# Attention four heads at a time in a fused attention, MoE and soft-MoE kernel

## The chip, the cores and the metric

The kernel runs on one core of one Trainium2 chip. The metric is device microseconds of one execution; three runs of the kernel before gave 681.8, 683.8 and 684.83, median 683.8.

## The reference

Three layers follow one another; the output of each is the input of the next:

```
# attention: batch 4, 12 heads, 448 positions, 64 wide
scores = cap * tanh(scale * q @ k.T / cap);  scores -= max(scores)
attn = exp(scores);  attn /= sum(attn) + 1e-9;  x = attn @ v      # -> 1792 tokens x 768
# MoE: 768 -> 2048 -> 768
h = x @ w_in;  g = s * relu(h)**2 + b;  x = g @ w_out
# soft MoE: 32 slots, 8 experts of 768 -> 1024 -> 768
logits = x @ phi;  d = softmax over tokens;  c = softmax over slots
slot_in = d.T @ x;  slot_out[e] = relu(slot_in[e] @ w1[e]) @ w2[e];  out = c @ slot_out
```

w_in and w_out arrive as 64-bit floats and are converted on the chip.

## The kernel before

The run has four stretches. In the **opening** the core computes attention of batch 0 and begins to convert weights. Then come four **blocks**, one for each batch: `block(bi)` multiplies the attention output x of batch bi by w_in (`hidden`, tile `hp`, 16 column chunks of 18 products each, in three terms of a high and a low part for accuracy), squares it, and folds it into the logits `L`, the transposed `g` and the running softmax (`post`, `chain`). Blocks 0 to 2 also carry the attention of the next batch, a step of it between any two pieces of `hidden`; block 3 has none. The **tail** reads 48 MB of expert weights (`wt`) and computes the soft MoE.

Attention works on a *pair* of heads at a time, 24 pairs, six for a batch. A pair has eight steps. Steps 0, 2, 4, 6 call `scores` for one of four chunks of 112 keys: six products into `sc` (two heads on 64 rows each, three terms), then a tanh on ScalarE (ACT) into `e`, and after each second chunk one exp over both chunks. `add` on VectorE (DVE) sums the four chunks of e into `es`, whose row 112 holds the 1e-9 of the denominator. In step 3 of the next pair `weighted` runs: two products of ones with `es` give the sums `Sm` (64 identical rows for each head), eight products of v with e give `U` (64 rows for each head, so the pair fills one bank of 128 rows). DVE then takes the reciprocal of Sm, multiplies U by it into `u`, and `split` writes u as a high part (a cast; on DVE in batch 0, on ACT later) and a low part (a subtraction on DVE) into x. Each fp32 product is two matmul records in the trace, so the eight U products are 16 records. `prep_pair` splits q and k in the same way.

PSUM has eight banks: L one, a shared bank "T" one (`bank`, used in turn by the transposes `tp` and `tw`, the projections `pp` and `pf` and the small tiles of `chain`; ACT or DVE must have copied one user out before PE writes the next), sc two, U one, Sm one, and two more that hold a second sc in the opening and `hp` in the blocks.

The order on each engine comes from a scheduler that starts from the order in the code. Every engine runs its own list in order, so an instruction that waits holds all behind it on that engine.

Of the kernel before, what the change touches and what calls it, by code (L numbers as in the profile page):

```python
# [17 lines left out]
P = 128  # L18
B, H, S, D = 4, 12, 448, 64
NP = H // 2  # L20
CP = 112
NCH = S // CP
DM = H * D
KC = DM // P
FF = 2048
# [9 lines left out]
EPS = 1e-9  # L35
CAP_FAST = 40.0
STEPS = 8
DIRECT = 0
CASTS = NP
LEAD = 4  # L40
U = 256
CU = 768
# [5 lines left out]
def load_qk(nc, io, p, q2, k2):  # L48

    nc.sync.dma_start(q2, io["qT"][p])  # L50
    nc.sync.dma_start(k2, io["kT"][p])


class Body:
    def __init__(self, nc, tc, io, consts, general, f64, wsc, osc):
        self.nc, self.tc, self.io, self.c, self.general = nc, tc, io, consts, general
        self.f64, self.wsc, self.osc = f64, wsc, osc
        self.ws, self.wr = {}, {}
        self.x = {}
        self.qk = {}  # L60
        self.r2 = {}
        self.e = {}
        self.u = {}
# [17 lines left out]
    def load_pair(self, p):  # L81
        if p >= B * NP or p in self.qk:
            return
        nc, io = self.nc, self.io
        if p < 2:
            q2, k2 = self.c["early"][p]
        else:
            q2 = self.ap.tile([P, S], F32, tag="q2", bufs=1, name="q2")
            k2 = self.ap.tile([P, S], F32, tag="k2", bufs=1, name="k2")
            load_qk(nc, io, p, q2, k2)  # L90
        v = self.ap.tile([CP, 2, NCH * D], F32, tag="v", bufs=3, name="v")
        nc.sync.dma_start(v, io["v"][2 * p:2 * p + 2].rearrange("i p d -> p i d"))
        self.qk[p] = (q2, k2, v)

    def prep_pair(self, p):
        if p >= B * NP:
            return
        q2, k2, v = self.qk[p]
        t = [self.ap.tile([P, S], F32R, tag=n, bufs=2, name=n) for n in ("qh", "ql", "kh", "kl")]
        self.split(t[0], t[1], q2, p)  # L100
        self.split(t[2], t[3], k2, p)
        self.qk[p] = (*t, v)

    def scores(self, p, c):

        nc = self.nc
        qh, ql, kh, kl, _ = self.qk[p]
        sc = (self.ps2 if self.ps2 is not None and c % 2 else self.psa).tile([CP, 2, 512], F32, tag="sc", bufs=1, name="sc")
        for j, (k, q) in enumerate(((kh, qh), (kh, ql), (kl, qh))):
            for i in range(2):  # L110
                r = slice(64 * i, 64 * i + 64)
                nc.tensor.matmul(sc[:, i, :S], k[r, c * CP:(c + 1) * CP], q[r, :], start=(j == 0), stop=(j == 2))  # L112
        if c % 2 == 0:
            self.e.setdefault(p, []).append(self.ap.tile([CP, 2, 2, S], F32, tag="e", bufs=3, name="e"))
        nc.scalar.activation(self.e[p][-1][:, :, c % 2, :], sc[:, :, :S], AF.Tanh, scale=self.c["tsc"][:CP])  # L115

    def chunk(self, g, c):

        return self.e[g // 2][c // 2][:, g % 2, c % 2, :]

    def greatest(self, g):
        nc, c = self.nc, self.c
# [17 lines left out]
    def expo(self, p, c):  # L140

        ready = [] if c % 2 == 0 else self.e[p][c // 2:]
        if self.general:
            ready = self.e[p] if c == NCH - 1 else []
            for i in range(2 if ready else 0):
                self.greatest(2 * p + i)
        for e in ready:
            self.nc.scalar.activation(e, e, AF.Exp, scale=self.c["acap"][:CP])  # L148

    def add(self, p, half):  # L150

        nc, es, e = self.nc, self.es[:CP], self.e[p][half]
        if half == 0:
            nc.vector.tensor_add(es, e[:, :, 0, :], e[:, :, 1, :])
        else:
            for k in range(2):
                nc.vector.tensor_add(es, es, e[:, :, k, :])  # L157

    def weighted(self, p):

        nc, c = self.nc, self.c
        U = self.psa.tile([P, 512], F32, tag="U", bufs=1, name="U")
        Sm = self.psa.tile([P, 512], F32, tag="S", bufs=1, name="Sm")
        v = self.qk[p][-1]
        for k in (3, 2, 1, 0) if p < DIRECT else ():
            for i in range(2):
                nc.tensor.matmul(Sm[64 * i:64 * i + 64, :S], c["ones"][:CP, :64], self.chunk(2 * p + i, k), start=(k == 3), stop=False)
        for i in range(2):
            nc.tensor.matmul(Sm[64 * i:64 * i + 64, :S], c["ones"][:CP + 1, :64], self.es[:CP + 1, i, :], start=(p >= DIRECT), stop=True)  # L169
        for k in range(NCH):  # L170
            for i in range(2):
                nc.tensor.matmul(U[64 * i:64 * i + 64, :S], v[:, i, k * D:(k + 1) * D], self.chunk(2 * p + i, k),  # L172
                                 start=(k == 0), stop=(k == NCH - 1))
        del self.qk[p], self.e[p]
        rec = self.ap.tile([P, S], F32, tag="rec", bufs=1, name="rec")
        nc.vector.reciprocal(rec, Sm[:, :S])  # L176
        u = self.ap.tile([P, S], F32, tag="u", bufs=1, name="u")
        nc.vector.tensor_mul(u, U[:, :S], rec)  # L178
        xt = self.xtile(p // NP)
        self.split(xt[:, 0, p % NP, :], xt[:, 1, p % NP, :], u, p)  # L180

    def xtile(self, bi):
        if bi not in self.x:
# [3 lines left out]

    def attention(self):

        for p in range(2):  # L190
            self.load_pair(p)
        self.prep_pair(0)
        self.es = self.ap.tile([P, 2, S], F32, name="es")
        self.nc.vector.memset(self.es, EPS)
        if not self.general:
            self.nc.vector.tensor_scalar(self.es, self.es, self.c["eps"], None, op0=ALU.mult)
        self.nc.vector.memset(self.es[:CP], 0.0)
        last = B * NP
        for p in range(last + 1):
            for k in range(STEPS):  # L200
                if p < last and k % 2 == 0:
                    if k == 0:
                        self.load_pair(p + 1)
                    self.scores(p, k // 2)
                    self.expo(p, k // 2)
                elif k == 3 and p:
                    self.weighted(p - 1)
                elif k in (5, 7) and p < last:
                    if p >= DIRECT and (k == 7 or not self.general):
                        for h in range(2) if self.general else (k // 7,):  # L210
                            self.add(p, h)
                    if k == 5:
                        self.prep_pair(p + 1)
                yield

    def convert(self, units):

# [65 lines left out]
    def conv_units(self):  # L283
# [510 lines left out]
def layouts(inputs):  # L794
    import numpy as np
    cc = np.ascontiguousarray
    q, k, v = inputs["q"], inputs["k"], inputs["v"]
# [18 lines left out]
    r = np.arange(P)  # L816
# [31 lines left out]
```

## Time and profile before

| | |
|---|---|
| median of three runs | 683.8 us |
| span of the profiled execution | 677.3 us |
| median of the runs over that span | 6.5 us |
| PE busy | 626.0 us (92%) |
| ACT busy | 416.2 us (61%) |
| DVE busy | 386.0 us (57%) |
| DMA reads and writes | 200 GB/s over the span |

The profile gives no time for its own execution beside the span, so the 6.5 us that lie around it are taken from the median. The averages hide that the stretches differ: the rows below give the engines' work by stretch.

### The profile page before, as it was taken

To read this page: it belongs to the slowest core of one execution; us is meant where nothing else is said; L and a number is where in the kernel's file an instruction comes from. 1 tells how busy PE (TensorE), PEld (TensorE's weight loads), DVE (VectorE), ACT (ScalarE), POOL (GpSimd) and SP (SyncE) were. 2 spreads that over 40 slices of the span, in tenths; PEclk is the share of its full clock that TensorE was granted. 3 is DMA by queue.
4 is the path that set the end of the run, shared out by engine and by line. 5 is a ranking of instruction groups with operands and counts; after the bars stand their busy time and mean duration, and the time that the engine had idled before them with its cause. 6 is when DMAs were issued, how large, how long until landed. Compare 5 with 4: busy or idle time off the path is not lost.

```text
span 677.3 us, 10643 instructions
## 1 busy us (share of the span) xinstructions
PE 626.0 (92%) x4234; PEld 403.8 (60%) x4234; DVE 386.0 (57%) x574; ACT 416.2 (61%) x688; POOL 4.0 (1%) x11
## 2 busy tenths in 40 slices
PE   4878999999999999999999999999999988987883
PEld 2323566666566666566566666667868864436773
DVE  6999998998785675745455655654332214101121
ACT  5959788986896877587768677776645550010011
POOL 1000000000000000000000000000000000000000
PEclk9979999999999999999999999999999998998887
DMA  7534468678485633132232232111977728999998
GB/s 230 195 101 144 153 246 289 219 271 280 172 276 198 215 98 107 51 94 80 74 99 74 75 91 72 46 47 47 370 269 282 274 92 337 420 419 417 418 412 309
DMA packets 43720, 136.55 MB, mean 202 GB/s; under 512 B 4352, under 2 KB 21264, under 8 KB 36752
## 3 DMA queue, kind: packets, MB, share of 16 engines
q1 hardware_dynamic: 43376, 135.28, 55.6%
q8 instruction: 35, 0.57, 0.4%
q0 software_dynamic: 288, 0.53, 0.2%
q14 instruction: 21, 0.17, 0.1%
HBM read 117.70 MB, written 18.09 MB: 200 GB/s over the span
## 4 chain that ended last, share of the span: by engine, by line
PE 69%; DMA 14%; DVE 10%; ACT 4%; issue 2%; SPq 0%; DVEq 0%
PE hp L385 32%; DMA wt<-in_w_dram 11%; PE U L172 10%; PE sc L112 8%; PE tp L400 4%; PE Sm L169 3%; DVE rec L176 2%; PE pt L474 2%; PE L L414 2%; PE tw L334 2%; DVE es L157 2%; DVE o L264 1%; ACT e L148 1%; PE si_ps L658 1%; PE idle L502 1%
## 5 line engine op out<-in xcount | busy, mean ns | idle before, releaser
L385 PE MATMUL hp<-x,ws 128*128 128x448 f32 x1152 | 278.1, 380 | 0.0
L385 PEld LDWEIGHTS hp<-x,ws 128*128 128x128 f32 x1152 | 204.3, 188 | 54.3 <-issue 40.5
L370 DVE TENSOR_TENSOR ws<-wr,ws 128x384 fp32r<-128x384 f32 x128 | 70.3, 554 | 99.7 <-ACT ws L369 96.7
L115 ACT ACTIVATE e<-sc,c_tsc 112x896 f32<-112x896 f32 x96 | 96.2, 1010 | 22.5 <-PE sc L112 22.1
L172 PE MATMUL U<-e,v 112*64 112x448 f32 x384 | 88.1, 552 | 9.9 <-DVE u L178 6.8
L369 ACT CAST ws<-wr 128x384 fp32r<-128x384 f32 x128 | 65.1, 514 | 37.8 <-PE hp L385 37.6
L148 ACT ACTIVATE e<-e,c_acap 112x1792 f32<-112x1792 f32 x48 | 86.2, 1797 | 0.4
L176 DVE RECIPROCAL rec<-Sm 128x448 f32<-128x448 f32 x24 | 70.9, 2954 | 16.3 <-PE Sm L169 15.3
L172 PEld LDWEIGHTS U<-e,v 112*64 112x64 f32 x384 | 29.5, 138 | 56.2 <-issue 48.3
L157 DVE TENSOR_TENSOR es<-es,e 112x896 f32<-112x896 f32 x48 | 52.2, 1087 | 18.3 <-ACT e L148 18.1
L402 ACT COPY g<-tp 112x256 f32<-112x256 f32 x128 | 42.0, 376 | 20.4 <-PE tp L400 19.7
L112 PE MATMUL sc<-qh,kh 64*112 64x448 f32 x192 | 46.0, 461 | 8.7 <-DVE kh L73 6.5
L390 ACT ACTIVATE r<-hp 128x448 f32<-128x448 f32 x64 | 34.6, 541 | 25.6 <-PE hp L385 25.4
L112 PEld LDWEIGHTS sc<-qh,kh 64*112 64x112 f32 x192 | 17.8, 176 | 44.2 <-issue 21.0
L400 PE MATMUL tp<-c_cst,r 128*112 128x128 f32 x256 | 38.9, 275 | 1.4 <-ACT r L391 1.2
L112 PE MATMUL sc<-ql,kh 64*112 64x448 f32 x192 | 39.5, 382 | 0.0
L722 ACT COPY wt<-op 128x512 f32<-128x512 f32 x12 | 7.0, 586 | 52.7 <-PE op L717 52.7
L112 PE MATMUL sc<-qh,kl 64*112 64x448 f32 x192 | 39.1, 381 | 0.4 <-DVE kl L74 0.4
L701 PE MATMUL so_ps<-wt,free 128*32 128x128 f32 x768 | 29.8, 303 | 10.0 <-DMA wt<-in_w_dram 10.0
L391 ACT ACTIVATE r<-r 128x448 f32<-128x448 f32 x64 | 37.3, 584 | 0.4
L400 PEld LDWEIGHTS tp<-c_cst,r 128*112 128x112 f32 x256 | 29.5, 133 | 10.5 <-ACT g L402 2.2
L701 PEld LDWEIGHTS so_ps<-wt,free 128*32 128x32 f32 x768 | 24.7, 122 | 14.1 <-DMA wt<-in_w_dram 12.7
(138 smaller groups left out, 581.8 us busy)
## 6 DMA issues: line engine op xcount, KB each, us to landing
wt<-in_w_dram SPq DMA_DIRECT2D x48, 1024.0 KB, 14.2
wr<-wsc SPq DMA_DIRECT2D x48, 384.0 KB, 3.1
raw<-in_w_in_dram SPq DMA_DIRECT2D x16, 768.0 KB, 4.4
raw<-in_w_outT_dram SPq DMA_DIRECT2D x16, 768.0 KB, 5.3
wsc<-wr SPq DMA_DIRECT2D x16, 384.0 KB, 3.2
osc<-o SPq DMA_DIRECT2D x24, 256.0 KB, 3.1
wt<-osc SPq DMA_DIRECT2D x6, 1024.0 KB, 7.3
v<-in_v_dram SPq DMA_DIRECT2D x24, 224.0 KB, 2.7
```

The source lines that it names most:

```text
L112: nc.tensor.matmul(sc[:, i, :S], k[r, c * CP:(c + 1) * CP], q[r, :], start=(j == 0), stop=(j == 2))
L115: nc.scalar.activation(self.e[p][-1][:, :, c % 2, :], sc[:, :, :S], AF.Tanh, scale=self.c["tsc"][:CP])
L148: self.nc.scalar.activation(e, e, AF.Exp, scale=self.c["acap"][:CP])
L157: nc.vector.tensor_add(es, es, e[:, :, k, :])
L172: nc.tensor.matmul(U[64 * i:64 * i + 64, :S], v[:, i, k * D:(k + 1) * D], self.chunk(2 * p + i, k), start=(k == 0), stop=(k == NCH - 1))
L176: nc.vector.reciprocal(rec, Sm[:, :S])
L369: self.nc.scalar.copy(hi, u)
L370: self.nc.vector.tensor_sub(lo, u, hi.bitcast(F32))
L385: nc.tensor.matmul(hp[:, :S], ws[kc // 3][:, w, kc % 3, :], x[:, s, kc, :], start=(k == 0), stop=(k == 3 * KC - 1))
L400: self.nc.tensor.transpose(tp[:CP, q * P:(q + 1) * P], r2[:, q * CP:(q + 1) * CP], self.c["idn"])
L402: self.nc.scalar.copy(self.g[q][:CP, :, fc * P:(fc + 1) * P], tp[:CP, 2 * q * P:2 * (q + 1) * P].rearrange("p (a b) -> p a b", b=P))
L701: nc.tensor.matmul(so_ps[32 * e:32 * e + 32, G, :], ht[G][:, f, 32 * e:32 * e + 32], w2[e // 2][:, e % 2, f, :], start=(f == 0), stop=(f = ...
```

## The change

Attention works on a *quad* of four heads, 12 quads, three for a batch, with 16 steps each.

- U is [128, 2, 512], two banks. Each head has 32 rows in each bank: its 64 columns of v are cut in two halves of 32. A quad has 32 U products of 32 columns in place of 2 x 8 of 64; the first two key chunks run at step 9, the last two in step 3 of the next quad. The rows of x are thereby in another order, and w_in's rows are laid out to match on the host.
- Sm is one tile for four heads, 32 rows each: four products of 32 columns in place of 2 x 2 of 64, and one reciprocal [128, 448] in place of two. Its own bank is gone; it uses the shared bank T. From quad 3 on ACT copies Sm out of T and the reciprocal works in place in SBUF.
- `finish`: U is multiplied by the reciprocal in place in PSUM, [128, 2 x 448] in one instruction; the high part is always cast by ACT from PSUM, [128, 896]; the low part is one subtraction of that size.
- e is one tile per key chunk, [112, 4 heads, 448], with three buffers as before; exp has the same size as before, and `add` is three instructions of 1792 in place of six of 896.
- es is set by GpSimd (POOL) instead of DVE. Pair 1's casts go to ACT. The split q and k have three buffers instead of two.

On DVE, in the opening, from a reciprocal on. Before (names: es sums of exp, x the output of attention, o and wr converted weights, ws split weights):

```order
L176 RECIPROCAL rec<-Sm 128x448
L154 TENSOR_TENSOR es<-e 112x896
L178 TENSOR_TENSOR u<-U,rec 128x448
L73 CAST qh<-q_313 128x448
L73 CAST x_273<-u 128x448
L74 TENSOR_TENSOR ql<-q_313,qh 128x448
L74 TENSOR_TENSOR x_273<-u,x_273 128x448
L73 CAST kh<-k_314 128x448
L157 TENSOR_TENSOR es<-es,e 112x896
L74 TENSOR_TENSOR kl<-k_314,kh 128x448
L157 TENSOR_TENSOR es<-es,e 112x896
```

Now, for four heads:

```order
L175 RECIPROCAL rec<-Sm 128x448
L75 TENSOR_TENSOR kl<-k_328,kh 128x448
L199 TENSOR_TENSOR U<-U,rec 128x2x448
L423 TENSOR_TENSOR ws<-wr,ws 128x384
L158 TENSOR_TENSOR es<-e 112x1792
L75 TENSOR_TENSOR x_371<-U,x_371 128x896
L74 CAST qh<-q_405 128x448
L74 CAST kh<-k_406 128x448
L75 TENSOR_TENSOR ql<-q_405,qh 128x448
L158 TENSOR_TENSOR es<-es,e 112x1792
```

One such row of rec, U and x now stands for two before, and the cast of x has left the engine.

On PE, in a block. Before, a pair's sums and products stand together (hp is the MoE product, tp a transpose into bank T):

```order
L400 MATMUL tp<-c_cst,r_1519 112x128 x4
L385 MATMUL hp<-x_894,ws 128x448 x2
L169 MATMUL Sm<-es,c_ones 64x448 x2
L172 MATMUL U<-e,v 64x448 x8
L385 MATMUL hp<-x_894,ws 128x448 x6
```

Now a quad's Sm stands in the row of users of bank T:

```order
L453 MATMUL tp<-c_cst,r_880 112x128 x4
L115 MATMUL sc<-qh,kh 112x448
L115 MATMUL sc<-ql,kh 112x448 x2
L115 MATMUL sc<-qh,kl 112x448
L172 MATMUL Sm<-es,c_ones 32x448 x4
L115 MATMUL sc<-qh,kl 112x448
L438 MATMUL hp<-x_371,ws 128x448 x3
L453 MATMUL tp<-c_cst,r_944 112x128 x4
```

and some runs of U are broken by other products:

```order
L189 MATMUL U<-e,v 32x448 x9
L369 MATMUL pp<-o,c_misc 32x256 x6
L189 MATMUL U<-e,v 32x448 x4
L387 MATMUL tw<-c_cst,o 128x128 x4
L189 MATMUL U<-e,v 32x448 x3
```

The Sm of a quad waits for tp before it to be copied out, and the tp behind it waits for the copy of Sm; and 9, 4 and 3 aren't multiples of four. In blocks 0 to 2 five runs of U are broken so by products that aren't Sm; before, three runs were.

The diff, cut to its core:

```
-    def split(self, hi, lo, src, p):
-        (self.nc.vector.tensor_copy if p < CASTS else self.nc.scalar.copy)(hi, src)
+    def split(self, hi, lo, src, vector):
+        (self.nc.vector.tensor_copy if vector else self.nc.scalar.copy)(hi, src)
...
+        t = [self.ap.tile([P, S], F32R, tag=n, bufs=2 if self.general else 3, name=n) for n in ("qh", "ql", "kh", "kl")]
+        self.split(t[0], t[1], q2, p < CASTS and p != 1)
...
+        if j == 0:
+            self.e.setdefault(Q, []).append(self.ap.tile([CP, 4, S], F32, tag="e", bufs=4 if self.general else 3, name="e"))
+        nc.scalar.activation(self.e[Q][c][:, 2 * j:2 * j + 2, :], sc[:, :, :S], AF.Tanh, scale=self.c["tsc"][:CP])
...
+    def add(self, Q, c):
+        es, e = self.es[:CP], self.e[Q]
+        self.nc.vector.tensor_add(es, e[0] if c == 1 else es, e[c])
...
+            self.Sm = self.psl.tile([P, 512], F32, tag="L", bufs=1, name="Sm") if direct else self.bank("Sm")
...
+        for i in range(4):
+            nc.tensor.matmul(self.Sm[32 * i:32 * i + 32, :S], c["ones"][:CP + 1, :32], self.es[:CP + 1, i, :], start=not direct, stop=True)
+        rec = self.ap.tile([P, S], F32, tag="rec", bufs=1, name="rec")
+        if Q < NQ:
+            nc.vector.reciprocal(rec, self.Sm[:, :S])
+        else:
+            nc.scalar.copy(rec, self.Sm[:, :S])
+            nc.vector.reciprocal(rec, rec)
...
+            self.U = self.psa.tile([P, 2, 512], F32, tag="U", bufs=1, name="U")
+        for k in chunks:
+            for h in range(2):
+                for i in range(4):
+                    nc.tensor.matmul(self.U[32 * i:32 * i + 32, h, :S], self.v[2 * Q + i // 2][:, i % 2, k * D + 32 * h:k * D + 32 * h + 32],
+                                     self.chunk(4 * Q + i, k), start=(k == 0), stop=(k == NCH - 1))
...
+    def finish(self, Q):
...
+        u = self.U[:, :, :S]
+        nc.vector.tensor_mul(u, u, self.rec[:, None, :].to_broadcast([P, 2, S]))
+        self.split(hi, lo, u, False)
...
+        self.nc.gpsimd.memset(self.es, EPS)
...
+                if not self.general and Q and s in (1, 3) and not (s == 1 and Q - 1 < DIRECT):
+                    if s == 1:
+                        self.add(Q - 1, 3)
+                    else:
+                        self.sums(Q - 1, (2, 3))
+                        self.weighted(Q - 1, (2, 3))
+                        self.finish(Q - 1)
...
+            if s == 9:
+                if Q < DIRECT:
+                    self.sums(Q, (0, 1))
+                self.weighted(Q, (0, 1))
+            if s in (9, 13) and Q >= DIRECT:
+                self.add(Q, 1 if s == 9 else 2)
...
+    wi = wi.reshape(NQ, 4, 2, D // 2, FF).transpose(0, 2, 1, 3, 4)
```

DIRECT is 0, so the branches for it don't run. The code for a large cap (`general`) is not taken in these runs.

## Rows read from the trace of the kernel before

**Rows 1.** Busy time of the engines by stretch: stretch, length, busy (instructions), granted clock.

```profile
6.00:81.00 75.00, 61.25 (x320) 27.89 (x321) 71.86 (x93) 57.19 (x57) 0.00 (x0) 0.93 0.51 165
81.00:410.00 329.00, 325.67 (x1849) 206.96 (x1849) 230.27 (x321) 253.28 (x423) 0.54 (x1) 1.00 0.47 157
410.00:555.00 145.00, 143.71 (x803) 107.32 (x801) 58.04 (x90) 91.06 (x183) 0.00 (x0) 1.00 0.45 164
555.00:677.00 122.00, 95.39 (x1270) 61.61 (x1267) 24.19 (x63) 13.15 (x25) 0.54 (x1) 0.86 0.97 391
```

**Rows 2.** DVE in order of time, at the opening's start and end: start, us.

```profile
7.24 0.81 DVE L194 MEMSET es<- 128x896 f32 x1
14.64 1.08 DVE L154 TENSOR_TENSOR es<-e 112x896 f32<-112x896 f32 x1
74.80 2.95 DVE L176 RECIPROCAL rec<-Sm 128x448 f32<-128x448 f32 x1
80.79 0.62 DVE L74 TENSOR_TENSOR x<-u,x 128x448 fp32r<-128x448 f32 x1
```

**Rows 3.** Groups by line and shape: busy us, mean ns, idle before and releaser.

```profile
L176 DVE RECIPROCAL rec<-Sm 128x448 f32<-128x448 f32 x24 | 70.9, 2954 | 16.3 <-PE Sm L169 15.3 <-PE U L172 1.1
L157 DVE TENSOR_TENSOR es<-es,e 112x896 f32<-112x896 f32 x48 | 52.2, 1087 | 18.3 <-ACT e L148 18.1
L178 DVE TENSOR_TENSOR u<-U,rec 128x448 f32<-128x448 f32 x24 | 14.7, 613 | 0.9 <-PE U L172 0.8
L74 DVE TENSOR_TENSOR x<-u,x 128x448 fp32r<-128x448 f32 x24 | 14.9, 621 | 8.0 <-ACT x L73 7.6
L73 DVE CAST x<-u 128x448 fp32r<-128x448 f32 x6 | 2.3, 386 | 0.0
L73 ACT CAST x<-u 128x448 fp32r<-128x448 f32 x18 | 10.1, 564 | 9.2 <-DVE u L178 8.9
L115 ACT ACTIVATE e<-sc,c_tsc 112x896 f32<-112x896 f32 x96 | 96.2, 1010 | 22.5 <-PE sc L112 22.1
L148 ACT ACTIVATE e<-e,c_acap 112x1792 f32<-112x1792 f32 x48 | 86.2, 1797 | 0.4
```

**Rows 4.** POOL in order of time: its last instruction in the opening.

```profile
3.48 0.54 POOL L776 DMA_DIRECT2D c_misc<-in_phi_dram  x1
```

**Rows 5.** The chain that ended last: start, us until the next piece, records.

```profile
302.98 0.90 PE Sm L169 x4
303.89 3.01 PE U L172 x16
308.31 0.89 PE L L414 x8
379.41 3.57 PE pt L474 x32
```

**Rows 6.** PE in order of time around a broken run.

```profile
321.47 0.97 PE L169 MATMUL Sm<-es,c_ones 113*64 113x448 f32 x2
322.37 0.46 PE L112 MATMUL sc<-qh,kh 64*112 64x448 f32 x2
...
323.16 0.59 PE L169 MATMUL Sm<-es,c_ones 113*64 113x448 f32 x1
...
327.07 0.67 PE L385 MATMUL hp<-x,ws 128*128 128x448 f32 x2
```

**Rows 7.** Waits: who for whom, us in total, times, longest us.

```profile
PE U L172 <- DVE u L178: 6.8, 3, 4.8
PEld pf L324 <- ACT o L336: 2.6, 5, 1.1
PEld tp L400 <- ACT g L402: 2.2, 6, 0.4
```

More of the change, by code (lines that the diff above doesn't have):

```diff
@@ L20 @@
 NP = H // 2
+NQ = H // 4
 CP = 112
@@ L62, in __init__ @@
         self.e = {}
-        self.u = {}
+        self.v = {}
         self.nslot = 0
@@ L83, in load_pair, with load_v @@
             return
-        nc, io = self.nc, self.io
         if p < 2:
[L86 to L93, printed above, removed]
+            self.qk[p] = self.c["early"][p]
+            return
+        self.qk[p] = [self.ap.tile([P, S], F32, tag=n, bufs=1, name=n) for n in ("q2", "k2")]
+        load_qk(self.nc, self.io, p, *self.qk[p])
+    def load_v(self, p):
+        if p >= B * NP or p in self.v:
+            return
+        self.v[p] = self.ap.tile([CP, 2, NCH * D], F32, tag="v", bufs=3, name="v")
+        self.nc.sync.dma_start(self.v[p], self.io["v"][2 * p:2 * p + 2].rearrange("i p d -> p i d"))
     def prep_pair(self, p):
@@ L147, in expo @@
         for e in ready:
             self.nc.scalar.activation(e, e, AF.Exp, scale=self.c["acap"][:CP])
[L150 to L154, printed above, removed]
-        else:
[L156 to L180, printed above, removed]
@@ new lines, in add, with sums @@
+    def add(self, Q, c):
+        es, e = self.es[:CP], self.e[Q]
+        self.nc.vector.tensor_add(es, e[0] if c == 1 else es, e[c])
+    def sums(self, Q, chunks):
+        nc, c = self.nc, self.c
+        direct = Q < DIRECT
+        if chunks[0] == 0 or not direct:
+            self.Sm = self.psl.tile([P, 512], F32, tag="L", bufs=1, name="Sm") if direct else self.bank("Sm")
+        for k in chunks if direct else ():
+            for i in range(4):
+                nc.tensor.matmul(self.Sm[32 * i:32 * i + 32, :S], c["ones"][:CP, :32], self.chunk(4 * Q + i, k), start=(k == 0), stop=False)
+        if chunks[-1] != NCH - 1:
+            return
+        for i in range(4):
[3 more added lines that the diff above has]
+            nc.vector.reciprocal(rec, self.Sm[:, :S])
+        else:
+            nc.scalar.copy(rec, self.Sm[:, :S])
+            nc.vector.reciprocal(rec, rec)
+        self.rec = rec
@@ new lines, in weighted @@
+    def weighted(self, Q, chunks):
+        nc = self.nc
+        if chunks[0] == 0:
+            self.U = self.psa.tile([P, 2, 512], F32, tag="U", bufs=1, name="U")
+        for k in chunks:
+            for h in range(2):
+                for i in range(4):
+                    nc.tensor.matmul(self.U[32 * i:32 * i + 32, h, :S], self.v[2 * Q + i // 2][:, i % 2, k * D + 32 * h:k * D + 32 * h + 32],
+                                     self.chunk(4 * Q + i, k), start=(k == 0), stop=(k == NCH - 1))
@@ L182, in xtile @@
+    def finish(self, Q):
+        nc = self.nc
+        xt = self.xtile(Q // NQ)
+        k = 2 * (Q % NQ)
+        hi, lo = (xt[:, s, k:k + 2, :] for s in range(2))
+        u = self.U[:, :, :S]
+        nc.vector.tensor_mul(u, u, self.rec[:, None, :].to_broadcast([P, 2, S]))
+        self.split(hi, lo, u, False)
+        del self.e[Q], self.v[2 * Q], self.v[2 * Q + 1]
     def xtile(self, bi):
@@ L188, in attention @@
     def attention(self):
-        for p in range(2):
-            self.load_pair(p)
+        self.load_pair(0)
+        self.load_pair(1)
+        self.load_v(0)
         self.prep_pair(0)
-        self.es = self.ap.tile([P, 2, S], F32, name="es")
-        self.nc.vector.memset(self.es, EPS)
+        self.prep_pair(1)
+        self.load_v(1)
+        self.es = self.ap.tile([P, 4, S], F32, name="es")
+        self.nc.gpsimd.memset(self.es, EPS)
         if not self.general:
-            self.nc.vector.tensor_scalar(self.es, self.es, self.c["eps"], None, op0=ALU.mult)
@@ L197, in attention @@
[L197 to L213, printed above, removed]
-                yield
+            self.nc.gpsimd.tensor_scalar(self.es, self.es, self.c["eps"], None, op0=ALU.mult)
@@ new lines, in attention @@
+        if DIRECT:
+            self.nc.gpsimd.memset(self.es[:CP], 0.0)
+        last = B * NQ
+        for Q in range(last + 1):
+            for s in range(2 * STEPS):
+                if Q < last:
+                    if s % 2 == 0:
+                        c, j = divmod(s // 2, 2)
+                        self.scores(2 * Q + j, c)
+                        if j:
+                            self.expo(Q, c)
+                    self.between(Q, s)
+                if not self.general and Q and s in (1, 3) and not (s == 1 and Q - 1 < DIRECT):
[5 more added lines that the diff above has]
+                        self.finish(Q - 1)
+                yield
@@ new lines, in between @@
+    def between(self, Q, s):
+        if s == 0:
+            self.load_pair(2 * Q + 2)
+        if s == 4:
+            self.load_v(2 * Q + 1)
+            self.load_v(2 * Q + 2)
+        if s == (13 if self.general else 7):
+            self.prep_pair(2 * Q + 2)
+            self.load_pair(2 * Q + 3)
+        if s == 15:
+            self.prep_pair(2 * Q + 3)
+        if self.general:
+            if s == 14:
+                for k in range(1, NCH) if Q >= DIRECT else ():
+                    self.add(Q, k)
+                self.sums(Q, range(NCH))
+                self.weighted(Q, range(NCH))
+                self.finish(Q)
+        else:
[5 more added lines that the diff above has]
+                self.add(Q, 1 if s == 9 else 2)
```

34 lines of the change are left out of this document (16 added, 18 removed).

## The prediction

> **What bounds the kernel now.** I read the busy time by stretch first, since the change touches only attention and the averages of the whole run hide where that stands. The reader is to see three limits in it [rows 1]. In the opening (6 to 81 us) DVE is busy 71.86 of 75 us (96%), PE 61.25, ACT 57.19: DVE is the limit. From 81 to 555 PE is busy 325.67 + 143.71 = 469.4 of 474 us, with DVE at 70% and then 40%: PE is the limit. From 555 on DMA is (0.97 busy). So DVE work counts in the opening, PE work in the blocks; what ends the blocks earlier moves the tail, which starts when they free its buffers, earlier by as much. Second, the timeline of DVE [rows 2]: the last reciprocal of batch 0 starts at 74.80, and the last subtraction into x ends at 80.79 + 0.62 = 81.4; block 0 can't finish its first column chunk without it. Third, the groups by shape for the durations [rows 3], the chain for the pitch of matmul runs [rows 5], and the waits on the PSUM banks [rows 7].
>
> **The opening.** Three quads take the place of six pairs. DVE, from [rows 3], the memset of es from [rows 2]:
> - reciprocals: 3 fewer x 2.954 = -8.9 us;
> - casts of x: 6 x 0.386 = -2.3, to ACT;
> - es is set by POOL: at least two memsets of 0.81 = -1.6;
> - an instruction of twice the columns: 448 to 896 takes the subtraction from 0.621 to the 1.087 of the same-shaped add, so 0.47 for each 448 more. Adds: 18 x 1.087 = 19.6 become 9 x (1.087 + 0.94) = 18.2, -1.3. Multiplications 6 x 0.613 = 3.7 become 3 x 1.08 = 3.2, subtractions 6 x 0.621 = 3.7 become 3 x 1.09 = 3.3: -0.9 together. That a PSUM operand and a PSUM result at 896 cost no more than this no row shows; even 0.5 us on each of the six would be 3 us.
>
> Sum -15. The new order splits one pair more ahead of the boundary, about 1.2 on DVE, so DVE has 71.9 - 14 = 58 us in the opening. ACT gains: three casts [128, 896] from PSUM at about 1.0 (the tanh of that size, 1.01), two casts of pair 1 and two of the extra pair at 0.564 each: 57.2 + 5.3 = 62.5. ACT is then the longest, from 6 us on: no end before 68.5. DVE as the limit lost 4% to waits; two engines near one another lose more, and there is a new hand-over. U is one buffer, and from a quad's last exp it is free only after add 2.0, sums 0.9, reciprocal 2.95, multiplication 1.1, cast 1.0, subtraction 1.1 = 9 us, while ACT has two chunks of the next quad ahead of it, 2 x (2 x 1.0 + 1.8) = 7.6, and a few casts. I count 1 us for each of two hand-overs and 3 us of other waits: the end comes at about 73.5 in place of 81.4. **-8**, bounds: -13 (ACT never waits) and -3 (ACT waits 10 us). Less than the 14 us taken from DVE, because ACT stands right behind it.
>
> POOL's two instructions on es are not in the trace. POOL is free from 4.0 us [rows 4], and the first add into es stood at 14.64 [rows 2] and can't come earlier now, as it needs eight tanhs and two exps where it needed four and one. DVE would need 2 x (0.81 + 0.68) = 3 us; up to 10.6 it costs nothing. I take 0, bounds 0 and +3.
>
> **The blocks.** Quads 3 to 11, nine of them, run where PE is the limit. A pair takes 0.90 + 3.01 = 3.91 us of PE [rows 5], a quad's worth 7.82. The change's shape stands in the trace at two places: L is four products of 32 columns over 448, eight records, in 0.89: so Sm for four heads takes 0.89 where it took 1.80. pt is 16 products of 32 columns, 112 rows and 512 moving columns in 3.57 us; times 448/512 that is 3.12 for 16 products of U, 6.25 for a quad against 6.02. Per quad 7.14 against 7.82: -0.68, times nine **-6.1**.
>
> Whether four column groups keep each other's pace decides this term. In the rows they do [rows 5]: pt's 32 records take 0.112 us each, 0.098 at 448 columns, where a record of the two-group U takes 3.01/16 = 0.188 and one alone would take 0.376. A rule of the Trainium skill speaks against it: "TensorE: Matmul & The Clock Gate", section "Part 3: Packing small matmuls — row/col tiling", says that four packed tiles measured 3.07 times one, and three column tiles 2.38 times. By that page a record would take 0.376/3.07 = 0.122 and the quad more than two pairs, and the estimate for the run would be 686. I take pt's row, whose shape is U's but for the columns; the other case is among the rivals.
>
> Three things are taken off or added.
> - Broken runs. Five of the new U runs are cut at a place that is no multiple of four by other products, against three before. [rows 6] show what a cut costs: Sm and U with scores between them take 327.07 - 321.47 = 5.60, less 0.79 for the scores (322.37 to 323.16) 4.81, against 3.91: 0.90. Two more cuts, less some cuts of Sm that are gone: **+1**, bounds 0 and +5 x 0.9.
> - Bank T. Behind Sm in PE's order stand pf or tp, which wait for ACT's copy of Sm; before it a tp or tw. The nearest rows are PE's waits for copies out of T: 2.6 us in 5 waits for pf, 2.2 in 6 for tp [rows 7], out of some 100 uses. Nine more uses with some 0.1 each: **+1**. From the other side, ACT can be in an exp (1.80) whenever PE gets there; nine times that and the copy (0.55) is 21.
> - PE waited 6.8 us in three waits for u to free U's bank [rows 7], and loses 4.6 in all from 81 to 555 [rows 1]. In the blocks a quad's U begins several hp runs after the former one's subtraction, since six steps of the attention lie between; **-0.5**.
>
> ACT's nine copies of Sm (0.55 each) and its larger casts add 5 us to the 344 of 474 that it is busy, DVE loses some 4 us a quad: neither becomes the limit. The tail has none of it.
>
> **Sum.** -8 - 6.1 + 1 + 1 - 0.5 = -12.6 on the profile's span of 677.3, so 664.7; the three runs lie 6.5 above the span by their median, and I take that as fixed: 671.2, so **671 us**, 1.9% faster.
>
> **Rivals.**
> - *The opening gives back most*: the hand-over of U and ACT's 62 us of work swallow it, and it ends at 78 instead of 73.5. For it speaks that a quad's finishing chain is 9 us against 5 for a pair, and that e has three buffers for four chunks, so a tanh of chunk 3 waits for U; against it the 14 us that DVE, the engine that bound, no longer has to do. -3 - 4.6 = -7.6: 676.
> - *More than that*: ACT hides its waits under the conversion work, -13, and no wait on T, -6: 665.
> - *Four groups don't run abreast in U.* pt uses one weight tile for all four groups; U has four of v and four moving tiles. If only three keep pace, a record takes 0.376/3 = 0.125: U 8.0 and Sm 1.0 are 9.0 a quad, +1.2 instead of -0.68, nine times +10.8. -8 + 10.8 + 1.5 = +4.3: 688, on the edge of what can be told from no change.
> - *The end on the other side: bank T becomes PE's wait.* Sm, tp, tw, pf and pp all go through one bank, and each next user needs ACT, which runs exps of 1.80 in its list. If each of the nine Sm holds PE by 1.8 before and 1.2 behind, that is +27 where I count 1: -12.6 + 26 = +13, 697. It costs the gain from about 1.4 us more for each Sm, and shows as slower from 1.8. Against it: the longest wait of tp for a copy was 0.4 [rows 7], and the new order puts ACT's copy right behind the copies of the tp before it.
>
> **How the numbers follow.** Less than 0.5% (3.4 us) can't be told from no change in runs that spread by 3 us; that is between 680.4 and 687.2. Chances: forecast 0.56, the opening gives back 0.19, more 0.12, four groups not abreast 0.07, bank T 0.06. Of the second some 0.04 lies above 680.4, of the fourth some 0.04 below 687.2. So faster is 0.56 + 0.15 + 0.12 = 0.83, the same 0.08, slower 0.03 + 0.06 = 0.09. The range leaves out the last two cases and the ends of the second and third: 663 to 679. The bounds of the single terms (opening -13 to -3, cuts 0 to +4.5, POOL 0 to +3) lie within it, unless several fall on one side together.
>
> **What would show it.** In the profile after, the opening's end (the last subtraction into x of batch 0) stands near 73.5, with ACT busier than DVE there; twelve reciprocals of 2.95; 32 records of U in 3.1 to 3.2 us of the chain, and 8 of Sm in 0.9; PE still busy over 98% from there to the end of the blocks, and that stretch about 4 to 5 us shorter; the tail as long as now. The prediction is wrong if a run of U takes over 3.5 us, if PE's waits for the copies of Sm or for bank T come to more than 5 us, or if the opening ends after 78.

## The result, and the profile after

The changed kernel takes 690.7 us (median of 4 runs, 688.79 to 692.73) against 682.8 us for the kernel before beside it (4 runs, 679.28 to 684.83): ratio 1.0124, 95% interval 1.0094 to 1.0155. It is 1.2% slower where 1.9% faster was forecast. The profiled execution spans 688.9 us where it spanned 677.3, a difference of 11.6 where the medians give 7.9. In all other runs the time lies 1.7 to 2.0 us above the span, so the trace of the kernel before is of its shortest run (679.28, 3.5 below its median) and that of the changed kernel of one at its median. So the 6.5 us set around the span ahead of the prediction are mostly this difference, and a difference of 2 or 3 us between two single traces may lie between executions and not between kernels.

The busy time by stretch, with stretches moved to where the work now is (columns as in [rows 1]: stretch, length, busy us and instructions of PE, PEld, DVE, ACT, POOL, then granted clock, DMA share and GB/s):

```profile
6.00:83.00 77.00, 60.92 (x415) 25.47 (x415) 64.81 (x68) 61.72 (x64) 5.68 (x2) 0.91 0.58 181
83.00:218.00 135.00, 131.09 (x841) 83.05 (x840) 100.81 (x131) 111.90 (x173) 0.00 (x0) 1.00 0.70 237
218.00:236.00 18.00, 11.87 (x62) 6.86 (x62) 14.17 (x13) 12.26 (x16) 0.00 (x0) 0.76 0.33 102
236.00:422.00 186.00, 184.76 (x1191) 114.55 (x1187) 90.28 (x131) 132.44 (x232) 0.60 (x1) 1.00 0.29 88
422.00:567.00 145.00, 143.36 (x864) 107.38 (x860) 52.70 (x80) 91.62 (x183) 0.00 (x0) 1.00 0.46 165
567.00:689.00 122.00, 91.26 (x1267) 57.44 (x1266) 24.16 (x63) 13.17 (x25) 0.54 (x1) 0.90 0.97 391
```

Two rows stand out. In the opening DVE no longer fills the stretch (64.81 of 77, against 71.86 of 75 in [rows 1]), yet no engine fills it in its place. And there is a stretch of 18 us in which PE is busy for 11.87 and its clock falls to 0.76, inside the blocks, where PE was always full.

To see where time came and went, I take from the timeline the start of the first relu of each block, that is, the moment at which the first `hp` chunk of a batch is done (us):

| kernel | block 0 | block 1 | block 2 | block 3 | span |
|---|---|---|---|---|---|
| before | 85.7 | 222.4 | 361.9 | 481.6 | 677.3 |
| after | 87.1 | 235.6 | 373.3 | 493.2 | 688.9 |
| difference | +1.4 | +13.2 | +11.4 | +11.6 | +11.6 |

At the last chunk of block 0 the difference was still +1.2 (214.6 and 215.8). So, in these two traces, the opening gained nothing, a loss of 12 us stands at the boundary of blocks 0 and 1 (called the stop below), and the rest of the run is as long as it was.

**The opening.** POOL's instructions on es in order of time (start, us; answers [rows 4]):

```profile
5.07 1.59 POOL L218 MEMSET es<- 128x1792 f32 x1 [1.02 <-DVE c_eps L818]
6.76 5.03 POOL L220 TENSOR_SCALAR es<-es,c_eps 128x1792 f32<-128x1792 f32 x1
```

DVE at the start and end of the opening, in order of time (in brackets: idle before, and what ended it; answers [rows 2]):

```profile
5.26 1.65 DVE L74 CAST qh<-c_tmp 128x448 fp32r<-128x448 f32 x1 [0.59 <-DMA c_tmp<-in_qT_dram]
6.83 0.37 DVE L74 CAST kh<-c_tmp 128x448 fp32r<-128x448 f32 x1
7.12 3.85 DVE L75 TENSOR_TENSOR ql<-c_tmp,qh 128x448 fp32r<-128x448 f32 x1
10.89 0.61 DVE L75 TENSOR_TENSOR kl<-c_tmp,kh 128x448 fp32r<-128x448 f32 x1
...
81.68 1.09 DVE L75 TENSOR_TENSOR x<-U,x 128x896 fp32r<-128x896 f32 x1 [1.22 <-ACT x L74]
```

The cast that ran beside POOL's memset took 1.65 us where the same cast otherwise takes 0.37 to 0.39, and the subtraction beside POOL's scaling took 3.85 where it otherwise takes 0.61. Both stand ahead of the first tanh: PE waited 2.96 us for ql within the first scores, and the first tanh started at 12.32 instead of 7.92. x of batch 0 is complete at 81.68 + 1.09 = 82.8, not at 73.5.

**The stop.** The last quad of batch 1, on PE in order of time (the rows of `hp` before 226 and most others are left out):

```profile
192.91 0.62 PE L377 MATMUL pf<-c_cst,c_tmp 128*128 128x32 f32 x4
...
219.01 0.60 PE L453 MATMUL tp<-c_cst,r 128*112 128x128 f32 x4
220.57 0.96 PE L172 MATMUL Sm<-es,c_ones 113*32 113x448 f32 x8
...
226.18 0.46 PE L115 MATMUL sc<-qh,kh 64*112 64x448 f32 x2 [2.41 <-ACT e L118]
...
231.96 1.11 PE L438 MATMUL hp<-x,ws 128*128 128x448 f32 x2 [2.35 <-ACT x L74]
233.34 2.23 PE L438 MATMUL hp<-x,ws 128*128 128x448 f32 x5 [0.27 <-DVE x L75]
```

and what DVE did for that quad:

```profile
189.51 2.01 DVE L158 TENSOR_TENSOR es<-es,e 112x1792 f32<-112x1792 f32 x1
...
226.19 2.95 DVE L178 RECIPROCAL rec<-rec 128x448 f32<-128x448 f32 x1
...
229.87 1.10 DVE L199 TENSOR_TENSOR U<-U,rec 128x896 f32<-128x896 f32 x1
...
232.19 1.09 DVE L75 TENSOR_TENSOR x<-U,x 128x896 fp32r<-128x896 f32 x1
```

es is ready at 191.5, but PE reaches Sm at 220.57: twelve other users of bank T (the first and the last of them are shown; the expectation of the first experiment counts eight) stand ahead of it in PE's list. From Sm on every step is the one that all wait for, and each stands behind other work: ACT copies Sm at 221.92 (behind an exp), DVE starts the reciprocal at 226.19 (behind an add of 2.02 and three conversions) and the multiplication at 229.87 (behind one more), and only then can ACT cast x, at 231.00. x is complete 12.7 us after Sm started, while PE has only scores left, which wait for e, and the first products of block 1, which wait for x. In the kernel before, es of batch 1's last pair was ready at 199.63, Sm stood at 200.35, in a bank of its own, x was complete at 210.6, and block 1 began without a wait (the kernel before, DVE and PE):

```profile
198.55 1.08 DVE L157 TENSOR_TENSOR es<-es,e 112x896 f32<-112x896 f32 x1
200.35 0.97 PE L169 MATMUL Sm<-es,c_ones 113*64 113x448 f32 x4
209.95 0.63 DVE L74 TENSOR_TENSOR x<-u,x 128x448 fp32r<-128x448 f32 x1
```

The clock pays a second time. The stretch in 10 us pieces (columns as above):

```profile
210.00:220.00 10.00, 9.55 (x62) 6.62 (x61) 0.78 (x2) 7.74 (x17) 0.00 (x0) 1.00 0.65 209
220.00:230.00 10.00, 6.10 (x36) 3.09 (x34) 7.70 (x7) 8.35 (x11) 0.00 (x0) 0.87 0.18 58
230.00:240.00 10.00, 7.77 (x36) 3.78 (x36) 7.72 (x9) 4.13 (x8) 0.00 (x0) 0.62 0.60 197
```

After PE's waits the granted clock is 0.87 and then 0.62, and five records of hp take 2.23 us at 233.34 where six take 1.42 at full clock (below). The two pieces hold 3.90 + 2.23 = 6.1 us of idle PE; 6.10 x 0.13 + 7.77 x 0.38 = 3.7 us more, as an estimate, went into a slower clock. That is 9.8 of the 12. The rest is work that stands here in PE's list: from the last relu of block 0 to the first of block 1 PE runs 73 records here, and 45 in the kernel before.

**The durations.** Groups by shape (busy us, mean ns, idle before and releaser; answers [rows 3]):

```profile
L199 DVE TENSOR_TENSOR U<-U,rec 128x896 f32<-128x896 f32 x12 | 13.1, 1092 | 0.2
L74 ACT CAST x<-U 128x896 fp32r<-128x896 f32 x12 | 10.9, 907 | 0.4 <-DVE U L199 0.4
```

The chain that ended last, around an unbroken run of U (start, us until the next piece, records; answers [rows 5]):

```profile
418.48 1.42 PE hp L438 x6
...
420.33 3.14 PE U L189 x32
```

Each single duration came out within 0.1 us of the forecast: 1.09 for the instructions of 896 columns, in PSUM too, 0.91 for ACT's cast (forecast 1.0), 0.53 for the copy, 0.89 from Sm's start to the next product (220.57 to 221.46 above), 3.14 for 32 of U.

### The profile page after: what moved, and what is told of

Its sections match the earlier page's. It is cut to its first block, busy times and chain, and to the rows that moved or that the text cites. A ratio compares the mean times of both kernels' runs of the same rounds, so it can differ in the third digit from the quotient of the medians.

```text
span 688.9 us, 11343 instructions
## 1 busy us (share of the span) xinstructions
PE 623.3 (90%) x4618; PEld 394.7 (57%) x4618; DVE 348.6 (51%) x491; ACT 424.6 (62%) x693; POOL 10.8 (2%) x13
## 4 chain that ended last, share of the span: by engine, by line
PE 63%; DMA 16%; ACT 11%; DVE 5%; issue 3%; SPq 0%; DVEq 0%; ACTq 0%
PE hp L438 30%; DMA wt<-in_w_dram 11%; PE U L189 10%; PE sc L115 7%; PE tp L453 4%; ACT e L118 4%; ACT e L153 3%; PE pt L527 2%; PE L L467 2%; DMA k<-in_kT_dram 1%; DMA raw<-in_w_in_dram 1%; DMA q<-in_qT_dram 1%; PE tw L387 1%; PE si_ps L711 1%; PE Sm L172 1%
## 5 line engine op out<-in xcount | busy, mean ns | idle before, releaser
L189 PE MATMUL U<-e,v 112*32 112x448 f32 x768 | 95.2, 562 | 1.9 <-ACT e L153 1.9
L115 PE MATMUL sc<-qh,kh 64*112 64x448 f32 x192 | 47.6, 470 | 20.2 <-ACT e L118 12.7
L158 DVE TENSOR_TENSOR es<-es,e 112x1792 f32<-112x1792 f32 x24 | 48.5, 2022 | 25.3 <-ACT e L153 25.2
L189 PEld LDWEIGHTS U<-e,v 112*32 112x32 f32 x768 | 25.2, 113 | 48.3 <-issue 42.1
L115 PE MATMUL sc<-ql,kh 64*112 64x448 f32 x192 | 41.0, 389 | 3.0 <-DVE ql L75 3.0
L115 PE MATMUL sc<-qh,kl 64*112 64x448 f32 x192 | 41.3, 386 | 0.7 <-DVE kl L75 0.7
L754 PE MATMUL so_ps<-wt,free 128*32 128x128 f32 x768 | 27.9, 283 | 13.6 <-DMA wt<-in_w_dram 13.6
L178 DVE RECIPROCAL rec<-rec 128x448 f32<-128x448 f32 x9 | 26.6, 2952 | 26.0 <-ACT rec L177 26.0
L158 DVE TENSOR_TENSOR es<-e 112x1792 f32<-112x1792 f32 x12 | 24.3, 2024 | 20.2 <-ACT e L153 20.2
```

Source lines behind the costliest of these rows:

```text
L158: self.nc.vector.tensor_add(es, e[0] if c == 1 else es, e[c])
L189: nc.tensor.matmul(self.U[32 * i:32 * i + 32, h, :S], self.v[2 * Q + i // 2][:, i % 2, k * D + 32 * h:k * D + 32 * h + 32], self.chunk(4 * ...
```

## The experiments

All ratios are to the kernel before on the same chip. In a diff, - is the kernel named first.

**b_sums_on_T**: the kernel before, with its sums in bank T and ACT's copy, nothing else.

```
-        Sm = self.psa.tile([P, 512], F32, tag="S", bufs=1, name="Sm")
+        Sm = self.bank("Sm")
...
+        if p < NP:
+            nc.vector.reciprocal(rec, Sm[:, :S])
+        else:
+            nc.scalar.copy(rec, Sm[:, :S])
+            nc.vector.reciprocal(rec, rec)
```

> One part of the change alone, on the kernel before: a pair's Sm takes its turn in bank T (and from batch 1 on ACT copies it out before the reciprocal); heads still go two at a time. Theory (turns of bank T): in the changed kernel the sums of the last quad of batch 1 had their es ready at 191.5 us but ran at 220.6, behind eight other users of T, so PE stood at the start of block 1 for x; the same should befall the last pair of batch 1 here: block 1's first relu (222.4 us before, 235.6 after) comes 6 to 12 us later than before, the run is 5 to 13 us slower than before (688 to 696). Rival (the longer finishing chain of four heads, or ACT's and DVE's load, makes x late, not the bank): within 2 us of before.

Measured: 693.85 us, ratio 1.0169 (1.0135 to 1.0203). First relus at 89.3, 236.4, 373.7, 494.7; span 688.5. PE in order of time around the last sums of batch 1:

```profile
225.32 0.97 PE L169 MATMUL Sm<-es,c_ones 113*64 113x448 f32 x4
...
233.81 0.67 PE L389 MATMUL hp<-x,ws 128*128 128x448 f32 x2 [0.47 <-ACT x L73]
```

The bank and ACT's copy alone, without quads, move the last Sm from 200.35 to 225.32, and the run is at least as slow as with the whole change. But PE waits only 0.47 us for x here: its list puts 20 other `hp` products between Sm and that wait, and PE's idle time is spread in small waits for pf, pp and u. So the late turn is shown, and that it must end in one stop is not. Nor is the price of the turn: from the first relu of block 0 to that of block 3 PE is busy for 400.6 of 405.4 us, and in the kernel before for 392.5 of 395.9, so most of the loss is busy time and not waiting. U alone is busy there for 70.9 us instead of 62.4, with the same products, in 42 pieces on PE's timeline instead of 27. And 3.6 us are lost ahead of block 0's first relu. What the late turn costs in the changed kernel has to come from the next two runs.

**a_sums_early**: in the changed kernel the last add and the sums are put at step 15 of the quad itself, the second half of U and `finish` stay at step 3 of the next.

```
-                    if s == 1:
-                        self.add(Q - 1, 3)
-                    else:
-                        self.sums(Q - 1, (2, 3))
+                if not self.general and Q < last and s == 15:
+                    self.add(Q, 3)
+                    self.sums(Q, (2, 3))
```

> The changed kernel with the last add and the sums of each quad called at its step 15 instead of steps 1 and 3 of the next quad: only the place of Sm in bank T's turns moves, four steps forward; U's second half and the multiplication stay. Theory (turns of T): the stop at block 1's start, some 11 us, goes for the most part, and the run is 680 to 684. Rival (finishing chain or load): less than 3 us faster than the changed kernel, 688 or more.

Measured: 685.89 us, ratio 1.0052 (1.0022 to 1.0082), some 2 us above what the theory expected. The last sums of batch 1 on PE:

```profile
212.65 0.96 PE L172 MATMUL Sm<-es,c_ones 113*32 113x448 f32 x8
```

x is complete at 221.5, and PE waits for neither. The difference to before is +4.4 us at block 0's first relu (the changed kernel has +1.4) and +6.5 at block 1's: the stop is gone, other small losses are not.

**a_lead12**: the changed kernel with LEAD = 12. `LEAD` (4 in both kernels) says how many of a block's 48 parts are left free of the next batch's attention at its end, so every quad is placed earlier.

> The changed kernel with LEAD 12 instead of 4: a block's share of attention is done by its 36th step of 48 and not its 44th, so sums, U's second half and finish of a batch's last quad all come earlier, bank T included. Theory (x is late at block 1's start because its finish is too late in the list): the stop goes, 679 to 685. If the stop at block 1 is of another kind (conversion of weights, DMA): no change, 689 to 692.

Measured: 680.47 us, ratio 0.9963 (0.9934 to 0.9992). The last sums of batch 1, and PE's only wait on their chain:

```profile
202.42 0.96 PE L172 MATMUL Sm<-es,c_ones 113*32 113x448 f32 x8
...
211.21 0.94 PE L189 MATMUL U<-e,v 112*32 112x448 f32 x2 [1.26 <-DVE x L75]
```

x is complete at 211.2, and block 1 waits for nothing (the 1.26 us are the next quad's U, which needs the bank); first relus at 89.4, 228.4, 366.4, 485.6. From block 0 to block 1 it takes 139.0 us, against 148.5 in the changed kernel and 136.7 before. That is 9.5 us gained in the place of the stop; its span is 7.3 shorter, since block 0 begins 2.3 us later.

**b_lead_twelve**: the same in the kernel before, as a control.

> The kernel before with LEAD at 12 instead of 4, so that the work of the next batch is spread over 36 instead of 44 parts of a block. A control for the run of the changed kernel with LEAD at 12, which took 10 us less than the changed kernel. Theory (what that run gained is the stop at the start of block 1, which the kernel before does not have): it gains nothing here, 681 to 686. Rival (a longer lead is good by itself, for the clock or for the order of the chunks): it falls by 4 to 10 us, to 673 to 679.

Measured: 687.59 us, ratio 1.0085 (1.0067 to 1.0104): slower, which neither view expected. A longer lead is no gain by itself in the kernel before, so what it gains in the changed kernel is put down to the stop, which its trace no longer has.

**a_es_on_dve**: the changed kernel with es filled and scaled on VectorE.

```
-        self.nc.gpsimd.memset(self.es, EPS)
+        self.nc.vector.memset(self.es, EPS)
...
-            self.nc.gpsimd.tensor_scalar(self.es, self.es, self.c["eps"], None, op0=ALU.mult)
+            self.nc.vector.tensor_scalar(self.es, self.es, self.c["eps"], None, op0=ALU.mult)
```

> The changed kernel with es set by DVE again (a memset and a multiplication of 1792 columns) and not by POOL. Theory (DVE's ql subtraction, 3.85 us instead of 0.62, and its first cast, 1.65 instead of 0.39, stood against POOL's two instructions on SBUF): they fall back to 0.4 and 0.6, first tanh at 8 to 9 us instead of 12.3, and the opening ends 2 to 4 us earlier; the run 687 to 689. Rival (late loads of q and k make them long): they stay long and nothing is gained, 690 to 692.

Measured: 683.23 us, ratio 1.0028 (1.0001 to 1.0056). DVE in order of time:

```profile
5.26 0.40 DVE L74 CAST qh<-c_tmp 128x448 fp32r<-128x448 f32 x1 [0.59 <-issue]
...
6.09 0.62 DVE L75 TENSOR_TENSOR ql<-c_tmp,qh 128x448 fp32r<-128x448 f32 x1
...
7.57 1.55 DVE L218 MEMSET es<- 128x1792 f32 x1 [0.32 <-issue]
...
10.04 1.15 DVE L220 TENSOR_SCALAR es<-es,c_eps 128x1792 f32<-128x1792 f32 x1
...
76.61 1.09 DVE L75 TENSOR_TENSOR x<-U,x 128x896 fp32r<-128x896 f32 x1 [1.44 <-ACT x L74]
```

With the same tiles and the same start (5.26), the cast takes 0.40 and the subtraction 0.62 again. DVE pays 1.55 + 1.15 = 2.7 us for es, and the opening still ends at 77.7 instead of 82.8, 5.1 earlier. The time is 4 us below the theory's range: the span is 8.2 shorter, more than the opening explains. Of the rest 2.0 lie in the tail (193.7 us from block 3's first relu to the end, instead of 195.7), which is between 193.5 and 196.2 in all thirteen traces; the ten runs of this kernel reach from 682.14 to 687.97, and the traced one took 682.56. The stop stays (block 0 to 1: 147.9 us).

**b_es_on_pool**: the other way round, the kernel before with es (half as large there) on POOL.

> The kernel before with its three instructions on es (fill, scale, fill with zero; 128x896, half the size of the changed kernel's) on GpSimd instead of VectorE. Theory (an instruction of GpSimd on a large tile stretches what VectorE runs beside it, as the 0.39 us cast took 1.65 and the 0.62 us subtraction 3.85 in the changed kernel): beside GpSimd's fill and scale, about 0.8 and 2.5 us, VectorE's first casts and subtractions of q and k take 2 to 6 times what they took, the first tanh starts at 8.5 to 10.5 instead of 7.92, and the time is 683 to 688. Rival (what was slow in the changed kernel came with its own tiles or waits, not from GpSimd): the casts take 0.39 and the subtractions 0.62, the first tanh starts at 7.9, and with 2.3 us less on VectorE the time is 679 to 683.

Measured: 683.5 us, ratio 1.0008 (0.9979 to 1.0037). POOL in order of time:

```profile
5.01 0.84 POOL L194 MEMSET es<- 128x896 f32 x1 [0.96 <-DVE c_eps L765]
5.96 2.75 POOL L196 TENSOR_SCALAR es<-es,c_eps 128x896 f32<-128x896 f32 x1
8.77 0.98 POOL L197 MEMSET es<- 112x896 f32 x1
```

and DVE:

```profile
5.21 0.89 DVE L73 CAST qh<-c_tmp 128x448 fp32r<-128x448 f32 x1 [0.59 <-DMA c_tmp<-in_qT_dram]
6.02 0.37 DVE L73 CAST kh<-c_tmp 128x448 fp32r<-128x448 f32 x1
6.32 1.35 DVE L74 TENSOR_TENSOR ql<-c_tmp,qh 128x448 fp32r<-128x448 f32 x1
...
8.12 0.84 DVE L73 CAST qh<-c_hh 128x448 fp32r<-128x448 f32 x1
8.88 1.11 DVE L73 CAST kh<-c_hh 128x448 fp32r<-128x448 f32 x1
```

The cast takes 0.89 instead of 0.39, the subtraction 1.35 instead of 0.62, and the first tanh starts at 9.01 instead of 7.92. The next pair's casts, 0.33 each in the kernel before, take 0.84 and 1.11. The stretching follows POOL into the other kernel; it costs less there, 0.7 us at block 0's first relu, and the time is that of the kernel before. That the 2.3 us less work on DVE make up for the rest is not shown.

**a_e_four**: the changed kernel with four buffers of e, and two instead of three of each split of q and k to make room.

> The changed kernel with four buffers of e instead of three, and two of each split of q and k instead of three, to make room. Theory (the rest of the opening that was not gained is ScalarE waiting for one of e's three buffers until the weighted products have read it, 5.9 us in three waits): those three waits go, x of batch 0 is complete 2 to 6 us earlier, and as the stop at the start of block 1 stays (about 12 us), the time falls by 2 to 6 us, to 685 to 689. Rival (ScalarE was full in any case, 61.7 of 77 us busy, and the wait for e only becomes a wait for the bank of the scores, or two buffers of the splits hold the casts back): the opening ends within 1 us of where it did, and the time stays at 689 to 692.

Measured: 692.09 us, ratio 1.0162 (1.0133 to 1.0191). What ACT waited for from 5 to 80 us (us in total, times, longest), in the changed kernel:

```profile
ACT e L118 <- PE sc L115: 7.3, 4, 3.6
ACT e L118 <- PE U L189: 4.1, 2, 2.9
```

and with four buffers:

```profile
ACT e L118 <- PE sc L115: 14.6, 8, 4.0
```

The wait for U to free e is gone, and came back as a wait for scores; x is complete at 83.2 instead of 82.8. So the three buffers of e are not what held the opening, and the time is the rival's. The stop is longer here (block 0 to 1: 154.0 us, against 148.5), which stays unexplained. That the two buffers of the splits took part of a gain can't be excluded.

**a_es_lead**: both edits that helped, es on VectorE and LEAD = 12; **a_es_lead_e** adds the buffers of a_e_four; **a_es_lead_8** and **a_es_lead_16** have LEAD at 8 and 16.

> The changed kernel with both edits that helped alone: es filled and scaled on VectorE, and LEAD at 12. Theory (they are two separate losses, 7.5 us at the start and 10 us at the start of block 1): the sum of both, 672 to 676. Rival (with a longer lead the opening's end does not reach the total, since the progress at the start of block 0 was no better than with LEAD at 4): 678 to 682.

> The changed kernel with es filled and scaled on VectorE, LEAD at 12 and four buffers of e (two of each split). Theory: 2 to 4 us less than with the first two edits alone, 669 to 674. Rival (the buffers of e were not what held ScalarE): within 1 us of it, 672 to 677.

> The changed kernel with es on VectorE and LEAD at 8. Theory (the stop at the start of block 1 goes only when the last quad's sums come at least some 20 us before its x is read, and each 4 of LEAD moves them by some 10 us): half of the stop stays, 672 to 679. Rival (the stop goes at once with any earlier place, and a longer lead costs by itself, as the kernel before with 12 shows): 668 to 672.

> The changed kernel with es on VectorE and LEAD at 16. Theory (the stop is gone at 12, and a longer lead only packs the next batch's work more tightly into the block): 672 to 678, not faster than at 12. Rival (some of the stop is left at 12): 667 to 671.

| kernel | us | ratio | interval | block 0 | block 1 | block 3 | span |
|---|---|---|---|---|---|---|---|
| a_es_lead | 671.97 | 0.9867 | 0.984 to 0.9895 | 81.3 | 218.2 | 475.0 | 670.3 |
| a_es_lead_e | 681.64 | 0.9997 | 0.9979 to 1.0015 | 88.6 | 231.1 | 488.4 | 683.2 |
| a_es_lead_8 | 674.17 | 0.9856 | 0.9826 to 0.9885 | 81.4 | 222.3 | 477.1 | 673.3 |
| a_es_lead_16 | 673.51 | 0.9891 | 0.9825 to 0.9957 | 82.5 | 221.4 | 478.0 | 671.5 |

(The blocks' columns are the first relus.) a_es_lead is 1.3% faster than the kernel before and, by the two ratios, 2.5% faster than the changed kernel: the two losses are separate and add up. Its busy time by stretch:

```profile
77.00:218.00 141.00, 137.70 (x875) 85.87 (x875) 108.73 (x136) 117.34 (x181) 0.00 (x0) 1.00 0.69 232
218.00:400.00 182.00, 181.53 (x1187) 112.47 (x1189) 94.34 (x135) 135.54 (x231) 0.54 (x1) 1.00 0.31 94
400.00:547.00 147.00, 146.54 (x880) 112.22 (x872) 54.20 (x83) 93.93 (x191) 0.00 (x0) 1.00 0.45 164
```

No stretch with a fallen clock is left in the blocks. The three values of LEAD can't be told apart by their intervals. At 8 the time is in the theory's range, but Sm runs at 210.2 and PE no longer waits for x, so I was wrong that half of the stop would stay: a few us earlier were enough. The changed buffers lost 10 us in a_es_lead_e; in its trace (685.05 us, the longest of its twelve runs) 7.3 are gone already at the first relu. I can't tell them apart further: it may be the two buffers, in place of three, of the splits.

## Why the prediction was wrong

Two terms failed: bank T and the opening. Between the two traces the result is +11.6 where -12.6 was forecast, 24.2 us apart: 9.4 in the opening and 14.8 in the blocks (forecast -4.6, measured 406.1 against 395.9 us from block 0's first relu to block 3's); of these 14.8 the stop is some 10, and the rest is the gain of the packing that didn't come. Of the signs that I had named the opening's end came (82.8, after 78); that of bank T did not, since it asked for another wait.

- **Bank T, forecast +1, cost some 10 to 12 us.** I priced each use of the bank as a short wait of PE for the copy, and there I was right: PE's waits at tp from 83 to 567 us come to 1.2 + 1.1 + 1.0 us, under the 5 that I had named as the sign. What I left out is that a bank handed round in a fixed order also fixes *where in PE's list* its users stand. Sm of the last quad stood 29 us behind its data, its chain of 12.7 us then ran over the boundary where block 1 needs x, and PE lost 6.1 us idle and an estimated 3.7 us by the clock. The trace names that wait "hp for x" and "scores for e", two and three links behind the cause. b_sums_on_T shows the late turn by itself, though not its price; a_sums_early and a_lead12 each remove the stop by placing the sums earlier, and b_lead_twelve shows that the earlier place is no gain of its own in the kernel before. My rival on bank T gave a time nearer to the result (697), by another mechanism: short waits at all nine Sm, which aren't there.
- **The opening, forecast -8, measured +1.4.** That POOL's work "up to 10.6 [...] costs nothing" was the first error. I asked when es is needed, and not what runs beside POOL: 1.26 us on a cast and 3.2 us on a subtraction, at the one place of the opening where PE and ACT have nothing else to do. a_es_on_dve gives back 5.1 us of the opening. What the rows show is that the cast ended at 6.91, 0.25 us behind the memset that it ran beside, that the next cast, at 6.83 beside the scaling, took 0.37, and that the subtraction ended 0.8 us before the scaling's recorded end. The Trainium skill has a rule for it ("SBUF — State Buffer", section "SBUF: two separate sides": VectorE and GpSimd share one port pair, which one of them holds for a whole instruction, against a VectorE instruction in a two-port mode, or one with two SBUF inputs if the GpSimd instruction reads SBUF). By that rule the first cast is explained; the second cast and the subtraction's end are not, unless POOL's recorded spans are off, which no run here settles. b_es_on_pool has the same pattern: three casts end 0.24 to 0.25 us behind a POOL instruction (at 6.10, 8.96 and 9.99, behind 5.85, 8.71 and 9.75), while the cast at 6.02 takes 0.37 and the subtraction ends 1.0 us before the scaling. The second error: without POOL the opening still ends at 77.7, not 73.5. ACT's work was as counted (61.72 against 62.5), its waits were not: 72 - 60.97 = 11 us idle from 6 to 78, where I took 5. They go round between scores, tanh and U (a_e_four moves one into the other). -3.7 is inside the bounds that I gave, close to the worst.
- **The blocks, forecast -6.1 and +1.** The forecast of the packing was right: 3.14 for 32 records of U (forecast 3.12), eight of Sm at the pace of L. The records take 0.098 us each (3.14 / 32), 3.8 times the pace of the 0.376 worked out for one alone (twice the 0.188 of two groups; no run has one alone). The figure of the Trainium skill that I had weighed against it ("TensorE: Matmul & The Clock Gate", section "Part 3: Packing small matmuls — row/col tiling": 3.07 times for four row tiles) is too low for this shape, four column groups of 448 columns each. But from the starts of successive groups of PE, blocks 0 to 2 give for Sm 14.7 to 7.4 us (-7.3, forecast -8.2) and for U 60.6 to 64.9 (+4.3, forecast +2.1 and the cuts), and scores, without the waits ahead of them, rise from 57.6 to 60.5 (59.5 in a_es_lead), which I had at 0. Cuts there are more than I counted: between these relus other products than Sm cut U at six places before and at fourteen now. What a cut costs stands in two rows of the changed kernel's PE:

```profile
240.29 0.96 PE L189 MATMUL U<-e,v 112*32 112x448 f32 x8
284.63 0.94 PE L189 MATMUL U<-e,v 112*32 112x448 f32 x2
```

The next group starts at 241.18 and 285.50, 0.89 and 0.87 us later: two records alone cost as much as eight. That the rise of the scores is a cost of cuts too is my guess; no run tests it. From the first relu of block 0 to that of block 3 PE is busy for 389.6 of 393.7 us in a_es_lead and for 392.5 of 395.9 before: 2.9 us less work, where the forecast was 5.1 less. Even that is not shown to be the packing's: b_es_on_pool, with the same 2210 records as before in another order, is busy for 397.6 of 400.2. The 7 us of span by which a_es_lead is shorter are 4.4 in the opening, 2.2 in the blocks and 0.4 in the tail.
- **The tail**, forecast as long as now: from block 3's first relu to the end 195.7 before and after. Right.

That a_es_lead lands at 672, where 671 was forecast, is no proof of the sum: the opening gives less, the blocks give less, and an earlier attention is in it that I had not reckoned with. So the agreement is luck.

## What to carry to other kernels

Moving a tile into a bank that others use in turn is priced by where its turn falls in the list, not by the wait at the bank: look for the last one before a boundary, follow its chain to whoever needs the result, and compare with the slack that the old bank gave. An idle engine is free for a small instruction only if nothing that matters runs beside it. When a saving on one engine uncovers no full engine behind it, count the hand-overs and not the work.

## What the runs showed of the hardware

- POOL's scaling of [128, 1792] took 5.03 us and its fill 1.59, where DVE took 1.15 and 1.55 for the same tile (a_es_on_dve); at [128, 896] POOL took 2.75 and 0.84.
- Beside them DVE's cast took 1.65 us instead of 0.39, and its subtraction of two SBUF tiles 3.85 instead of 0.62; with the tiles of half the size 0.89 and 1.35 (b_es_on_pool).
- 6 us of waits on PE at one place were followed by a granted clock of 0.62 over 10 us, that is, PE ran partly at 1.2 GHz, and cost an estimated 3.7 us on top.
- A piece of U with two records (one product of 32 columns) held PE for 0.87 us, a piece with eight (four such products) for 0.89 (changed kernel, at 284.63 and 240.29); 32 in one run took 3.14.
